# Linear attention feeding a gated MLP: features, keys and queries on half rows in pairs, TensorE in program order

## The chip, the cores and the metric

The kernel runs on one core of a Trainium2 chip. The metric is the device time of one execution in microseconds; lower is better. The core has five engines that run side by side and wait for each other through semaphores: TensorE (PE, with its weight loads shown apart as PEld), VectorE (DVE), ScalarE (ACT), GpSimd (POOL) and SyncE (SP). TensorE writes to PSUM, which has eight banks here; results are taken out of it by ScalarE or VectorE ("evacuated").

## The reference

Eight batches, eight heads, 576 positions, head size 64. First a linear attention with an exponential feature map, then an MLP with a spatial gate:

```python
def phi(x):
    proj = np.einsum('bhsd,df->bhsf', x, w_phi)             # 64 -> 128
    proj = proj - np.max(np.abs(proj), axis=-1, keepdims=True)
    return np.concatenate([np.exp(proj), np.exp(-proj)], axis=-1)
q_p, k_p = (phi(q), phi(k))
kv = np.einsum('bhsf,bhsd->bhfd', k_p, v)
z = np.sum(k_p, axis=2)
num = np.einsum('bhsf,bhfd->bhsd', q_p, kv)
den = np.einsum('bhsf,bhf->bhs', q_p, z)[..., None] + 1e-06
attn_out = num / den

x = attn_out.transpose(0, 2, 1, 3).reshape(B, S, 512)
h = np.maximum(x @ w_in, 0.0)                               # 512 -> 1024
u, v = h[..., :512], h[..., 512:]
v_n = (v - mean(v)) / np.sqrt(var(v) + 1e-06)
v_s = np.einsum('ts,bsd->btd', w_spatial, v_n) + b_spatial[None, :, None]
out = (u * v_s) @ w_out
```

## The kernel before

The attention works in *units*. A unit is one pair of heads of one batch over 512 positions (four blocks of 128), 32 in all, or, for two batches at a time, all eight heads over the last 64 positions (the *tail*), four in all. `step(i)` starts unit i and carries on with units started earlier, each part of the work at a fixed lag (`LAGS`): keys and queries at the unit's own step, maxima one step later, features and sums two later, attention three, output four.

- `a_transpose`: keys and queries with the head dimension on the partitions, two half rows (64 partitions each) one above the other. From batch 2 on a DMA does it (`cross`, tiles `kT_b`, `qT_b`).
- `a_keys` and `a_queries` call `by_token`: k or q times `w_phi`, positions on the partitions, one PSUM bank of 128x512 for each of two halves. `wphi2` is `w_phi` twice along a block diagonal, zeros elsewhere, so that one matmul over all 128 rows handles both half rows and gives 256 columns (L232). Of the keys VectorE takes the maximum of the absolute values (`mk`, L244) and ScalarE the exponentials with both signs (`kf`, L247). Of the queries VectorE takes the maximum (`mq`, L258), and GpSimd splits it into two bf16 parts (`mhl`, L261 and L262).
- `a_scale`: the key maximum becomes a factor `em` on v (`vs`, GpSimd, L272).
- `a_max_t`: `mhl` is transposed (L293) and copied to `mT` by VectorE (L294).
- `a_qfeat`: the query projection again, features on the partitions (L304; L313 for a tail), minus the maximum, which a matmul of the selection matrix `sel` with `mT` adds into the same bank (L308; L315). ScalarE takes both exponentials (`qf`, L321).
- `a_kv`: the sums over positions (L334, L336; evacuated as `kv`). `a_num`: numerator and denominator (L354), then division on VectorE (L344, L345) into `x`; `tail_num` does it for the tail (L382).
- `a_x_t`: the transpose of x, by a DMA for most units.

When a batch is complete, `b_tasks` appends its *second-stage tasks* to `queue`: v with the layer norm's statistics (`b_v`: matmuls L403, ScalarE relu L405, VectorE statistics L406, L407), the normalization on GpSimd (`b_ln`), u (`b_u`: L456, ScalarE relu L458), the spatial product (`b_s`: L477, L478, multiplied into u on VectorE, L480), and the output (`b_o`: L500, evacuated by ScalarE as `ob`, L502, written by a DMA of SP), and the same for tails. `fill(share)` adds `RATE * share` to a credit, up to `CAP`, and takes tasks off the queue while the credit covers half of the next task's cost, which is counted in us of TensorE (0.85 for four matmuls of 512 columns, 1.07 for five). The rest of the queue is emptied after the last step.

Engines and lines are chosen by the kernel. The order in which each engine's instructions stand is made by a scheduler from the order of the program, except where `tc.keep_in_program_order` holds an instruction to it. All PSUM tiles share one pool of eight banks; a tile waits for a bank whose last reader is done. The scheduler's order for the kernel before has, in a middle step on TensorE: maxima transpose, keys, a task, queries, a task, attention, sums, a task, features.

Of the kernel before, what the change touches and what calls it, by code (L numbers as in the profile page):

```python
# [16 lines left out]
def kernel(  # L17
# [15 lines left out]
    nc = tc.nc  # L33
# [23 lines left out]
    psum = ctx.enter_context(tc.tile_pool(name="psum", bufs=8, space=bass.MemoryType.PSUM))  # L57

# [65 lines left out]
    wphi2 = cpool.tile([P, 2 * F], BF16)  # L124
    pin(nc.vector.memset)(wphi2, 0.0)
# [14 lines left out]
    sel1 = cpool.tile([P, H], BF16)  # L140
    sel = cpool.tile([P, H, F], BF16)
    pin(nc.vector.tensor_tensor)(out=sel1, in0=ident[:, 0:H], in1=ident[:, H:2 * H], op=ALU.add)
    pin(nc.vector.tensor_scalar)(out=sel, in0=sel1.unsqueeze(2).to_broadcast([P, H, F]), scalar1=-1.0,
# [4 lines left out]
    for i in range(2):  # L148
        t = cpool.tile([P, 2, 2, H, DA], BF16, name=f"vst{i}")
        pin(nc.scalar.copy)(out=t.rearrange("p b s h d -> p (b s h d)"), in_=zero.to_broadcast([P, 4 * H * DA]))  # L150
        vst.append(t)
        if i == 0:
            for y in range(2):
                r = slice(y * D, (y + 1) * D)
                pin(nc.scalar.copy)(out=wphi2[r, y * F:(y + 1) * F], in_=wphi_f[r, :])
        t = cpool.tile([P, 2, HALF], BF16, name=f"vnt{i}")
        for bl, row in ((0, TL), (1, 0)):
            pin(nc.scalar.copy)(out=t[:, bl, :], in_=ident[:, row:row + 1].to_broadcast([P, HALF]))
        vnt.append(t)
# [24 lines left out]
    XX = 9  # L184
    EK = 7
    def transpose_spatial(i):

        pt = psum.tile([P, S], BF16, tag="bank", name="pt")
        if i < NB:
            sc = POS[i]  # L190
            for tp, c in enumerate(POS):
                nc.tensor.transpose(out=pt[:, tp * P:(tp + 1) * P], in_=wsp[:, c, bass.ds(sc, P, step=NB)],
                                    identity=ident)
            nc.tensor.transpose(out=pt[:, T0:S], in_=wspt[:, bass.ds(sc, P, step=NB)],
# [3 lines left out]
        for bl in range(2):  # L198
            lo = bl * TL
            for tp, c in enumerate(POS):  # L200
                nc.tensor.transpose(out=pt[lo:lo + TL, tp * P:(tp + 1) * P], in_=wspr[:, c, :], identity=ident)
            nc.tensor.transpose(out=pt[lo:lo + TL, T0:S], in_=wspt[:, T0:S], identity=ident[:TL, :TL])
# [9 lines left out]
    def a_transpose(u):  # L212
# [5 lines left out]
        for x, copy in (("k", nc.vector.tensor_copy if u["i"] < EK else nc.scalar.copy), ("q", nc.vector.tensor_copy)):  # L218
            pt = psum.tile([P, 4, P], BF16, tag="bank", name="pt")
            for j in range(4):  # L220
# [4 lines left out]
                nc.tensor.transpose(out=pt[:, j, :], in_=blk, identity=ident)  # L225
# [3 lines left out]
    def by_token(xT, half):  # L229
        ps = psum.tile([P, 4, F], FP32, tag="bank", name="ps")  # L230
        for x in range(2):
            nc.tensor.matmul(out=ps[:, 2 * x:2 * x + 2, :], lhsT=xT[:, 2 * half + x, :], rhs=wphi2,  # L232
                             start=True, stop=True)
        return ps

    def a_keys(u):

        u["mk"] = small.tile([P, H], FP32, tag="mk", name="mk")
        u["kf"] = feat.tile([P, 2, H, F], BF16, tag="kf" if u["pair"] else "kf_t", name="kf",
                            bufs=4 if u["pair"] else 2)  # L240
        for half in range(2):
            pk = by_token(u["kT"], half)
            hs = slice(4 * half, 4 * half + 4)
            nc.vector.tensor_reduce(out=u["mk"][:, hs], in_=pk, axis=AX.X, op=ALU.max,  # L244
                                    apply_absolute_value=True)
            for s, sc in ((0, 1.0), (1, -1.0)):
                nc.scalar.activation(out=u["kf"][:, s, hs, :], in_=pk, func=AF.Exp, bias=0.0, scale=sc)  # L247

    def a_queries(u):

        m, early = mhl[u["i"] % NM], u["i"] < EARLY
        if not early:
            mq = small.tile([P, H], FP32, tag="mq", name="mq")
        for half in range(2):
            pq = by_token(u["qT"], half)
            if early and half == 0:
                mq = pq[:, 0, 0:H]
            nc.vector.tensor_reduce(out=mq[:, 4 * half:4 * half + 4], in_=pq, axis=AX.X, op=ALU.max,  # L258
                                    apply_absolute_value=True)
        eng = nc.vector if early else nc.gpsimd  # L260
        eng.tensor_copy(out=m[:, 0:H], in_=mq)  # L261
        eng.tensor_tensor(out=m[:, H:2 * H], in0=mq, in1=m[:, 0:H], op=ALU.subtract)  # L262
# [28 lines left out]
    def a_max_t(u):  # L291
        pt = psum.tile([P, P], BF16, tag="bank", name="pt")
        nc.tensor.transpose(out=pt, in_=mhl[u["i"] % NM], identity=ident)  # L293
        nc.vector.tensor_copy(out=mT[u["i"] % NM][0:2 * H, :], in_=pt[0:2 * H, :])  # L294

    def a_qfeat(u):

        m = mT[u["i"] % NM]
        u["qf"] = []
        for half in range(2):  # L300
            pq = psum.tile([P, 4, P], FP32, tag="bank", name="pq")
            if u["pair"]:
                for par in range(2):
                    nc.tensor.matmul(out=pq[:, 2 * par:2 * par + 2, :], lhsT=wphi2[:, par * F:(par + 1) * F],  # L304
                                     rhs=u["qT"][:, 2 * half:2 * half + 2, :], start=True, stop=False)
                    for x in range(2):
                        j = 4 * half + 2 * x + par
                        nc.tensor.matmul(out=pq[:, 2 * par + x, :], lhsT=sel[:, j, :], rhs=m,  # L308
                                         start=False, stop=(x == 1))
            else:  # L310
                for x in range(4):
                    h = 4 * half + x
                    nc.tensor.matmul(out=pq[:, x, :], lhsT=wphi2[:, (h % 2) * F:(h % 2 + 1) * F],  # L313
                                     rhs=u["qT"][:, h // 2, :], start=True, stop=False)
                    nc.tensor.matmul(out=pq[:, x, :], lhsT=sel[:, h, :], rhs=m, start=False, stop=True)  # L315
            if u["pair"]:
                qf = feat.tile([P, 2, 4, P], BF16, tag="qf", name="qf", bufs=7)
            else:
                qf = feat.tile([P, 2, 4, P], BF16, tag="qf_t", name="qf_t", bufs=4)
            for s, sc in ((0, 1.0), (1, -1.0)):  # L320
                nc.scalar.activation(out=qf[:, s], in_=pq, func=AF.Exp, bias=0.0, scale=sc)  # L321
            u["qf"].append(qf)

    def a_kv(u):
# [5 lines left out]
        for hh in range(2):  # L330
            h = 2 * u["pj"] + hh
            for s in range(2):
                for c in range(NB):
                    nc.tensor.matmul(out=pv[:, hh, s, :], lhsT=u["kf"][:, s, 4 * hh + c, :],  # L334
                                     rhs=u["vs"][:, s, 4 * hh + c, :], start=(c == 0), stop=False)
                nc.tensor.matmul(out=pv[:, hh, s, :], lhsT=ut["kf"][:, s, h, :],  # L336
# [10 lines left out]
    def a_num(u):  # L347
        d = st[u["b"]]
        u["x"] = a1.tile([P, NB, 2, D], BF16, tag="x", name="x", bufs=3)
        for hh in range(2):  # L350
            pn = psum.tile([P, NB, DA], FP32, tag="bank", name="pn")
            for pos in range(NB):
                for s in range(2):
                    nc.tensor.matmul(out=pn[:, pos, :], lhsT=u["qf"][hh][:, s, pos, :],  # L354
# [3 lines left out]
    def a_x_t(u):  # L358
# [8 lines left out]
        for pos in range(NB):  # L367
            nc.tensor.transpose(out=pt[:, pos, :], in_=u["x"][:, pos].rearrange("p h d -> p (h d)"), identity=ident)
        nc.vector.tensor_copy(out=dst, in_=pt.rearrange("p n t -> p (n t)"))

    def tail_num(g, bls):
# [4 lines left out]
        for i in range(2):  # L376
            pn = psum.tile([P, 4, DA], FP32, tag="bank", name="pn")
            for y in range(4):
                for bl in bls:
                    r = slice(bl * TL, (bl + 1) * TL)  # L380
                    for s in range(2):
                        nc.tensor.matmul(out=pn[r, y, :], lhsT=qf[i][:, s, y, r],  # L382
# [5 lines left out]
    def tail_x_t(g, bls):  # L388
# [5 lines left out]
        for kc in range(KC):  # L394
            nc.tensor.transpose(out=pt[:, kc, r], in_=d["xt"][r, 2 * kc:2 * kc + 2, :].rearrange("p h d -> p (h d)"),
# [4 lines left out]
    def v_mm(lhs, dst, r, stats, mv):  # L400
        pv = psum.tile([P, HALF], FP32, tag="bank", name="pv")
        for kc in range(KC):
            nc.tensor.matmul(out=pv[r], lhsT=lhs(kc), rhs=w_in_bf[:, kc, HALF:DFF],  # L403
# [48 lines left out]
    def b_u(b, dc):  # L452
        d = st[b]
        pu = psum.tile([P, T0], FP32, tag="bank", name="pu")
        for kc in range(KC):
            nc.tensor.matmul(out=pu, lhsT=w_in_bf[:, kc, dc * P:(dc + 1) * P], rhs=d["xT"][:, kc, :],  # L456
# [3 lines left out]
    def b_u_tail(g, bls):  # L460
# [5 lines left out]
        for dc in range(KC):  # L466
            for kc in range(KC):
                nc.tensor.matmul(out=pu[:, dc, r], lhsT=w_in_bf[:, kc, dc * P:(dc + 1) * P],
# [215 lines left out]
```

## Time and profile before

| | |
|---|---|
| time before, three runs | 288.0, 289.58 (median), 291.42 us |
| span of the profiled execution | 286.4 us; what lies around it is not given |
| PE busy | 261.6 us (91%) |
| ACT busy | 229.3 us (80%) |
| DVE busy | 201.8 us (70%) |
| POOL busy | 182.2 us (64%) |
| granted TensorE clock | full throughout |

How to read it: busy time is the union of an engine's instructions, so overlapping ones count once, while the mean of a group is that of one instruction with its latency. The chain of waits follows the execution back from its last instruction, at each point to what released it. The timeline gives start, duration, engine, line, operation, output and input; a merged row has xN. Brackets name idle time ahead of an instruction and what ended it. The table by stretch gives the start and end of a stretch, its length, and then the busy time of PE, PEld, DVE, ACT and POOL with the number of instructions, the clock, the share of the DMA engines, and GB/s.

The span has four parts. Up to 18.7 us the first units are loaded and begun. From there to 49.4 us seven steps run with hardly any second-stage work. From 49.4 to 222.0 us lie 27 steps with second-stage tasks among them. The remaining 64.4 us hold the last steps, which have no new units, and the second stage of the last batches.

### The profile page before, as it was taken

Reading aid. Unit: us, or ns where it says so; the run is one execution under the profiler, and the core shown is the slowest. Engines: PE = TensorE matmul, PEld = TensorE weight load, DVE = VectorE, ACT = ScalarE, POOL = GpSimd, SP = SyncE. Lnnn points to the kernel's source line nnn. Section 1 sums busy time; section 2 is a strip of 40 time slices with the busy share of each in tenths; the row PEclk is TensorE's granted clock in tenths of the full one; section 3 lists DMA queues with packets and bytes.
Section 4 is the critical chain, followed back from the end, with each engine's and each line's share of the span. In section 5 each row is a group of like instructions: output and inputs, shape, how many; then the busy total and the mean of one; then the engine's idle time right before and its main releaser. Section 6 shows DMA issues by size and latency. Waiting matters only on the chain.

```text
span 286.4 us, 7965 instructions
## 1 busy us (share of the span) xinstructions
PE 261.6 (91%) x3070; PEld 178.6 (62%) x3070; DVE 201.8 (70%) x509; ACT 229.3 (80%) x517; POOL 182.2 (64%) x320
## 2 busy tenths in 40 slices
PE   1378889999999999999989999999999999999983
PEld 1157776777666776767557687666667676545441
DVE  4389997977958877598696887578688864354610
ACT  4949998899799988999998679799999746566033
POOL 8159998798336899479689954835969600058200
PEclk9999999999999999999999999999999999999999
DMA  6989999976568499999955994999111003500037
GB/s 185 203 171 120 206 219 223 163 203 71 79 147 186 102 187 155 173 245 196 130 94 102 225 191 87 264 287 255 32 22 32 7 2 122 211 3 0 0 90 242
DMA packets 81706, 40.31 MB, mean 141 GB/s; under 512 B 50242, under 2 KB 77058, under 8 KB 81668
## 3 DMA queue, kind: packets, MB, share of 16 engines
q1 hardware_dynamic: 54180, 28.32, 43.0%
q0 software_dynamic: 27328, 11.41, 35.5%
q8 instruction: 24, 0.39, 0.6%
q14 instruction: 14, 0.11, 0.2%
q10 hardware_dynamic: 160, 0.07, 0.1%
HBM read 32.85 MB, written 9.44 MB: 148 GB/s over the span
## 4 chain that ended last, share of the span: by engine, by line
PE 61%; ACT 14%; DVE 11%; DMA 9%; POOL 2%; issue 2%; ACTq 0%; SPq 0%; POOLq 0%; DVEq 0%
PE pv L403 10%; PE ps L477 8%; PE po L500 7%; PE pu L456 7%; PE ps L232 5%; ACT qf L321 5%; ACT kf L247 5%; PE pv L334 4%; DMA q_tl<-in_q_dram 4%; PE pn L354 4%; DMA out_dram<-ob 3%; PE pq L308 3%; PE pq L304 3%; DVE mk L244 3%; PE ps L478 2%; DVE mq L258 2%
## 5 line engine op out<-in xcount | busy, mean ns | idle before, releaser
L247 ACT ACTIVATE kf<-ps 128x512 bf16<-128x512 f32 x144 | 77.7, 692 | 5.6 <-DVE mk L244 5.4
L272 POOL TENSOR_TENSOR vs<-v_f,em 128x512 bf16<-128x512 f32 x64 | 65.6, 1049 | 23.6 <-ACT em L267 22.6
L321 ACT ACTIVATE qf<-pq 128x512 bf16<-128x512 f32 x128 | 68.2, 675 | 8.5 <-PE pq L308 8.5
L244 DVE TENSOR_REDUCE mk<-ps 128x4 f32<-128x512 f32 x72 | 46.1, 677 | 2.5 <-PE ps L232 2.0
L258 DVE TENSOR_REDUCE mq<-ps 128x4 f32<-128x512 f32 x62 | 39.9, 681 | 4.2 <-PE ps L232 3.4
L502 ACT COPY ob<-po 128x512 f32<-128x512 f32 (+1 forms) x37 | 21.6, 610 | 19.9 <-PE po L500 16.2
L406 DVE BATCH_NORM_STATS2 stats<-vr 128x6 f32<-128x512 bf16 (+1 forms) x37 | 24.8, 687 | 15.8 <-ACT vr L405 15.7
L477 PE MATMUL ps<-w_spT,vn 128*128 128x512 bf16 x128 | 32.8, 379 | 0.0
L456 PE MATMUL pu<-xT,w_in_bf 128*128 128x512 bf16 x128 | 31.6, 379 | 0.0
L403 PE MATMUL pv<-w_in_bf,xT 128*128 128x512 bf16 x128 | 31.2, 379 | 0.0
L480 DVE TENSOR_TENSOR uT<-ps,uT 128x512 bf16<-128x512 f32 x32 | 22.0, 689 | 12.7 <-PE ps L478 11.5
L500 PE MATMUL po<-w_out_bf,uT 128*128 128x512 bf16 x128 | 30.4, 379 | 0.0
L308 PE MATMUL pq<-mT,sel 128*128 128x128 bf16 x256 | 30.0, 219 | 0.0
L308 PEld LDWEIGHTS <-sel 128*128 128x128 bf16 x256 | 25.1, 98 | 3.9
L405 ACT ACTIVATE vr<-pv 128x512 bf16<-128x512 f32 (+1 forms) x37 | 23.3, 691 | 4.0 <-PE pv L403 3.9
L354 PEld LDWEIGHTS <-qf 128*128 128x128 bf16 x512 | 20.4, 97 | 8.2 <-issue 1.7
L345 DVE TENSOR_TENSOR x<-pn,rc 128x256 bf16<-128x256 f32 x64 | 25.0, 418 | 0.5
L420 POOL TENSOR_SCALAR vn<-vr,rs 128x512 bf16<-128x512 bf16 x32 | 24.3, 773 | 0.8
L334 PE MATMUL pv<-vs,kf 128*128 128x66 bf16 x512 | 24.5, 194 | 0.2 <-ACT kf L247 0.2
L354 PE MATMUL pn<-kv,qf 128*128 128x66 bf16 x512 | 22.3, 193 | 1.3 <-ACT qf L321 1.2
L334 PEld LDWEIGHTS <-kf 128*128 128x128 bf16 x512 | 21.7, 97 | 1.8 <-issue 0.9
L304 PE MATMUL pq<-qT_b,wphi 128*128 128x256 bf16 x96 | 22.4, 273 | 0.0
(120 smaller groups left out, 530.8 us busy)
## 6 DMA issues: line engine op xcount, KB each, us to landing
v_f<-in_v_dram SPq DMA_DIRECT2D x8, 1024.0 KB, 10.7
out_dram<-ob SPq DMA_DIRECT2D x32, 256.0 KB, 3.6
k_bf<-in_k_dram POOLq DMA_DIRECT2D x7, 512.0 KB, 7.0
q_bf<-in_q_dram POOLq DMA_DIRECT2D x7, 512.0 KB, 8.7
v_tl<-in_v_dram SPq DMA_DIRECT2D x8, 128.0 KB, 7.7
w_in_bf<-in_moe_w_in_dram POOLq DMA_DIRECT2D x2, 512.0 KB, 8.7
out_dram<-ob SPq DMA_DIRECT2D x8, 128.0 KB, 2.4
k_tl<-in_k_dram POOLq DMA_DIRECT2D x8, 64.0 KB, 6.8
```

The costliest lines, as they stand in the source:

```text
L244: nc.vector.tensor_reduce(out=u["mk"][:, hs], in_=pk, axis=AX.X, op=ALU.max, apply_absolute_value=True)
L247: nc.scalar.activation(out=u["kf"][:, s, hs, :], in_=pk, func=AF.Exp, bias=0.0, scale=sc)
L258: nc.vector.tensor_reduce(out=mq[:, 4 * half:4 * half + 4], in_=pq, axis=AX.X, op=ALU.max, apply_absolute_value=True)
L272: nc.gpsimd.tensor_tensor(out=vs[:, s, :, 0:D], in0=st[u["b"]]["v"][:, pj * H:(pj + 1) * H, :], in1=em[:, s, :].unsqueeze(2).to_broadcast( ...
L308: nc.tensor.matmul(out=pq[:, 2 * par + x, :], lhsT=sel[:, j, :], rhs=m, start=False, stop=(x == 1))
L321: nc.scalar.activation(out=qf[:, s], in_=pq, func=AF.Exp, bias=0.0, scale=sc)
L334: nc.tensor.matmul(out=pv[:, hh, s, :], lhsT=u["kf"][:, s, 4 * hh + c, :], rhs=u["vs"][:, s, 4 * hh + c, :], start=(c == 0), stop=False)
L354: nc.tensor.matmul(out=pn[:, pos, :], lhsT=u["qf"][hh][:, s, pos, :], rhs=d["kv"][:, 2 * u["pj"] + hh, s, :], start=(s == 0), stop=(s == 1))
L403: nc.tensor.matmul(out=pv[r], lhsT=lhs(kc), rhs=w_in_bf[:, kc, HALF:DFF], start=(kc == 0), stop=(kc == KC - 1))
L456: nc.tensor.matmul(out=pu, lhsT=w_in_bf[:, kc, dc * P:(dc + 1) * P], rhs=d["xT"][:, kc, :], start=(kc == 0), stop=(kc == KC - 1))
L477: nc.tensor.matmul(out=ps, lhsT=d["vn"][:, sp, cs], rhs=w_spT[:, sp, 0:T0], start=(sp == 0), stop=False)
L500: nc.tensor.matmul(out=po[r], lhsT=lhs(dc), rhs=w_out_bf[:, dc, :], start=(dc == 0), stop=(dc == KC - 1))
```

## The change

`wphi2` gives way to `wphi`, `w_phi` once on each half of the partitions without zeros. Each projection is a pair of matmuls over 64 rows, one on the upper and one on the lower half of the array's rows, into two different banks. Features, keys and queries of a step follow each other as one group (`p_features`, `p_keys`, `p_queries`), six banks together. In the features the `sel` matmuls come first and one matmul of 512 columns per half row follows. The selection matrix has four entries, repeated on both halves; `mT` is copied in all its rows. The blocks of a unit stand in a different order in `kf` and `qf`, which `slot` translates.

From step 8 (`STRICT`) on, every TensorE instruction is held to the order of the program. The evacuations of the group (`e_features`, `r_keys`, `e_keys`, `r_queries`) are called with four equal `fill(0.25)` among them and the other parts; the maxima's transpose comes last in a step, and the features first in the next. `RATE` goes from 3.12 to 3.35 and `CAP` from 2.11 to 2.5. `ob` is evacuated by VectorE, except after the last step (`drain`), when ScalarE does it as before.

```diff
+    strict = [False]
+    def on_pe(f, *a, **kw):
+        r = f(*a, **kw)
+        if strict[0]:
+            tc.keep_in_program_order(r)
+    def matmul(**kw):
+        on_pe(nc.tensor.matmul, **kw)
...
-    wphi2 = cpool.tile([P, 2 * F], BF16)
-    pin(nc.vector.memset)(wphi2, 0.0)
+    wphi = cpool.tile([P, F], BF16)
...
-    sel1 = cpool.tile([P, H], BF16)
-    sel = cpool.tile([P, H, F], BF16)
-    pin(nc.vector.tensor_tensor)(out=sel1, in0=ident[:, 0:H], in1=ident[:, H:2 * H], op=ALU.add)
+    sel1 = cpool.tile([P, 4], BF16)
+    sel = cpool.tile([P, 4, F], BF16)
+    pin(nc.vector.tensor_tensor)(out=sel1, in0=ident[:, 0:4], in1=ident[:, 4:8], op=ALU.add)
+    for i in (D, D + 4):
+        pin(nc.vector.tensor_tensor)(out=sel1, in0=sel1, in1=ident[:, i:i + 4], op=ALU.add)
...
-    def by_token(xT, half):
-        ps = psum.tile([P, 4, F], FP32, tag="bank", name="ps")
-        for x in range(2):
-            nc.tensor.matmul(out=ps[:, 2 * x:2 * x + 2, :], lhsT=xT[:, 2 * half + x, :], rhs=wphi2,
-                             start=True, stop=True)
-        return ps
+    HALVES = (slice(0, D), slice(D, P))
+    def banks(name):
+        return [psum.tile([P, 4, P], FP32, tag="bank", name=name) for par in range(2)]
+    def by_token(xT, name):
+        outs = banks(name)
+        for y in range(4):
+            for par, r in enumerate(HALVES):
+                matmul(out=outs[par][:, y, :], lhsT=xT[r, y, :], rhs=wphi[r, :], start=True, stop=True)
+        return outs
+    def p_features(u):
+        m = mT[u["i"] % NM]
+        u["pf"] = pf = banks("pf")
+        for y in range(4):
+            for par, r in enumerate(HALVES):
+                matmul(out=pf[par][:, y, :], lhsT=sel[r, y, :], rhs=m[r, :], start=(y == 0), stop=False)
+        for par, r in enumerate(HALVES):
+            matmul(out=pf[par], lhsT=wphi[r, :], rhs=u["qT"][r], start=False, stop=True)
+    def e_features(u):
+        u["qf"] = qf = feat.tile([P, 2, 8, P], BF16, tag="qf" if u["pair"] else "qf_t", name="qf",
+                                 bufs=3 if u["pair"] else 2)
+        for par in range(2):
+            for s, sc in ((0, 1.0), (1, -1.0)):
+                nc.scalar.activation(out=qf[:, s, 4 * par:4 * par + 4, :], in_=u["pf"][par], func=AF.Exp,
+                                     bias=0.0, scale=sc)
...
-        nc.vector.tensor_copy(out=mT[u["i"] % NM][0:2 * H, :], in_=pt[0:2 * H, :])
+        nc.vector.tensor_copy(out=mT[u["i"] % NM], in_=pt)
...
-        nc.scalar.copy(out=ob[r], in_=po[r])
+        (nc.scalar.copy if drain[0] else nc.vector.tensor_copy)(out=ob[r], in_=po[r])
...
-    ORDER = (("keys", 0.375), ("queries", 0.25), ("attention", 0), ("sums", 0.25),
-             ("next", 0.125), ("features", 0), ("out", 0), ("maxima", 0))
-    RATE = 3.12
-    CAP = 2.11
+    RATE = 3.35
+    CAP = 2.5
...
+        strict[0] = i >= STRICT
+        run("features", p_features)
+        run("keys", p_keys)
+        run("queries", p_queries)
+        run("features", e_features)
+        run("keys", r_keys, lambda u: e_keys(u, 0))
+        fill(0.25)
+        run("queries", r_queries)
+        run("keys", lambda u: e_keys(u, 1), a_scale)
+        fill(0.25)
+        for u in at_work("attention"):
+            a_num(u)
+            if u["pj"] == NP - 1:
+                finish_batch(u, tail_num)
+        fill(0.25)
+        run("sums", a_kv)
+        run("next", a_transpose)
+        fill(0.25)
+        for u in at_work("out"):
+            a_x_t(u)
+            if u["pj"] == NP - 1:
+                finish_batch(u, tail_x_t)
+                queue.extend(b_tasks(u["b"]))
+        run("maxima", a_max_t)
```

`r_keys` and `r_queries` are the two VectorE reductions of `a_keys` and `a_queries` over both banks (with `mhl` split by GpSimd as before), and `e_keys(u, par)` the two ScalarE exponentials of one bank. The old loop over `ORDER` in `step`, which called the parts and then `fill(share)`, is removed.

## The prediction

> **What bounds the kernel now.** I read, in this order: busy time per engine with the chain that ended last, busy time by stretch, the groups by line with shapes kept apart, the timeline of one step.
>
> ```profile
> PE 261.6 (91%) x3070; PEld 178.6 (62%) x3070; DVE 201.8 (70%) x509; ACT 229.3 (80%) x517; POOL 182.2 (64%) x320
> PE 61%; ACT 14%; DVE 11%; DMA 9%; POOL 2%; issue 2%; ACTq 0%; SPq 0%; POOLq 0%; DVEq 0%
> ```
>
> TensorE holds 61% of the chain, but ScalarE and VectorE follow at 80% and 70%. By stretch (length, then busy time of PE, PEld, DVE, ACT, POOL):
>
> ```profile
> 49.40:222.00 172.60, 169.19 (x2110) 119.55 (x2109) 135.47 (x335) 157.90 (x372) 126.71 (x228) 1.00 0.90 151
> 222.00:286.40 64.40, 59.18 (x534) 33.12 (x531) 29.00 (x67) 32.07 (x61) 17.24 (x32) 1.00 0.23 75
> 18.70:49.40 30.70, 26.47 (x393) 21.42 (x392) 28.10 (x81) 27.78 (x68) 29.27 (x44) 1.00 1.17 179
> ```
>
> In the middle, 27 steps between copies of mT, TensorE works 169.2 of 172.6 us. A step takes 172.6/27 = 6.4 us. VectorE has 37 us to spare, ScalarE 15.
>
> The groups that the change rewrites, and the evacuations that it re-orders (mean ns last):
>
> ```profile
> L247 ACT ACTIVATE kf<-ps 128x512 bf16<-128x512 f32 x144 | 77.7, 692 | 5.6 <-DVE mk L244 5.4
> L244 DVE TENSOR_REDUCE mk<-ps 128x4 f32<-128x512 f32 x72 | 46.1, 677 | 2.5 <-PE ps L232 2.0
> L308 PE MATMUL pq<-mT,sel 128*128 128x128 bf16 x256 | 30.0, 219 | 0.0
> L304 PE MATMUL pq<-qT_b,wphi 128*128 128x256 bf16 x96 | 22.4, 273 | 0.0
> L232 PE MATMUL ps<-wphi,qT_b 128*128 128x256 bf16 x96 | 14.5, 273 | 1.4 <-DMA qT_b<-q_bf 1.4
> L232 PE MATMUL ps<-wphi,kT_b 128*128 128x256 bf16 x96 | 14.4, 272 | 0.0
> ```
>
> These means overlap. I use pace: four L232 matmuls take 0.44 us in the chain (0.11 each), eight of 512 columns 1.73 (0.216 each), ScalarE's exponentials come 0.49 apart, VectorE's reductions 0.60 apart.
>
> One step in time order decides the forecast:
>
> ```profile
> 121.49 0.22 PE L293 MATMUL pt<-ident,mhl 128*128 128x128 bf16 x1
> 121.55 0.60 PE L232 MATMUL ps<-wphi,kT_b 128*128 128x256 bf16 x4
> 121.62 0.69 DVE L406 BATCH_NORM_STATS2 stats<-vr 128x6 f32<-128x512 bf16 x1 [2.23 <-ACT vr L405]
> 122.23 0.19 DVE L294 COPY mT<-pt 16x128 bf16<-16x128 bf16 x1
> 122.45 1.26 DVE L244 TENSOR_REDUCE mk<-ps 128x4 f32<-128x512 f32 x2
> 126.14 0.27 PE L304 MATMUL pq<-qT_b,wphi 128*128 128x256 bf16 x1
> ```
>
> Maxima are transposed at 121.49 and copied at 122.23. TensorE never waits: it starts keys at 121.55, and the features that read mT only at 126.14. That copy has nearly 4 us of slack, and the key matmuls lie between it and VectorE's next work.
>
> [...]
>
> ```profile
> 53.57 0.39 PE L192 MATMUL pt<-ident,wsp 128*128 128x128 bf16 x4
> 53.89 0.22 PE L194 MATMUL pt<-ident,wspt 64*128 64x64 bf16 x1
> 54.04 0.41 PE L192 MATMUL pt<-ident,wsp 128*128 128x128 bf16 x4
> ```
>
> Four at 0.055 us end their turn at 53.79; the 64-row one starts at 53.89, the next group 0.15 later: about 0.1 us per switch. [...] no 64-row pair is in this trace. [...]
>
> **The change part by part.**
>
> *Half rows in pairs.* Keys and queries: each 4 x 0.11 = 0.44 becomes 4 pairs x 0.055 = 0.22. Features: 4 x 0.11 + 8 x 0.055 = 0.88 becomes 4 pairs of sel x 0.055 + one pair of 512 columns 0.216 = 0.44. Saved: 0.88 a step if pairs overlap fully, nothing if they don't (the low bound); two switches take 0.2. I take a net 0.65 a step: 27 x 0.65 = 18 us in the middle.
>
> *The new wait.* In the built order every step from STRICT on reads: last second-stage task, maxima transpose, features, keys, queries; features begin with sel on mT. So TensorE waits for transpose (0.22), VectorE's copy (0.20) and two handovers (0.04 seen from pt to copy; about 0.1 back): 0.56 at least. VectorE's copy stands behind its evacuation of the step's last task wherever that is a spatial product or an output: 0.60 more, less what passes during the transpose, so about 1.1. Mean 0.85 a step, x 27 = 23 us. Behind it queue all TensorE work; VectorE's next instruction, mk, waits for keys behind features: 0.1 + 0.1 + 0.22 + 0.22 + 0.22 + 0.2 of pipeline = about 1.05 us idle each step. Slack is gone, and TensorE and VectorE take turns.
>
> *More tasks per step.* RATE 3.12 to 3.35 gives TensorE 0.23 more a step: 27 x 0.23 = 6 us in the middle. Late, the built order shows a spatial task, a spatial tail and one output fewer after the last maxima (1.07 + 1.2 + 0.86 = 3 us).
>
> *Outputs on VectorE.* 19 of the middle's steps' ob copies move. Their price there isn't shown: L227 (417 ns, bf16) bounds it below, L480 (689) above; I take 0.60, 11.4 us onto VectorE, some 10 off ScalarE. ScalarE's relief hides nothing by itself; VectorE's cover is the 37 us, which turn-taking consumes.
>
> *Middle, three sums.* TensorE: 169 - 18 + 6 + 23 = 180 to 182. VectorE: 135.5 + 11.4 + 2 for the extra tasks + 27 x 1.05 = 177. Neither is alone: a step with four layer-norm tasks asks VectorE for 2.4 + 1.0 + 0.13 + 4 x 0.7 + 1.05 = 7.3 us, and its statistics wait for ScalarE, which in the built order gives vr only after the key exponentials; a step with four uT tasks asks ScalarE for 12 x 0.49 + 0.75 = 6.6. Before, a heavy step ran on into a light one. Going through the 27 steps of the built order, taking each one's dearest engine, I get 186: 13.4 more than 172.6.
>
> *Early* (7 steps, not strict but in the same order): VectorE is busy 28.1 of 30.7, and 1.05 idle a step replaces about 0.4; with TensorE's gain I take +3 (bounds 0 and +5). *Late*: -3 of tasks, -0.9 for the features of two steps, +1 of waits: -3.
>
> *At nothing*: sel and wphi (one 0.29 us copy and half of a 0.72 us scaling less; the k_tl transfer, waited for until 12.89, covers them; uncovered, below 1 us); the mT copy of 128 rows for 16 (same columns); qf as one tile. No DMA changes in number. SP's order changes only in how outputs lie among xT transposes; POOL keeps its order of work, and the mhl that maxima read has a whole step. PSUM: six banks held could stall kv until the first key bank is free; by the built banks ScalarE frees it 3.8 us into a step, TensorE needs it at 4.3, so no cost; if ScalarE is late, up to 1 us a step.
>
> Sum: 286.4 + 13.4 + 3 - 3 = 299.8 us of span. What lies around the profiled span isn't given; the median shown, 289.58, is 3.2 above it. Some of the DMA waits of before (4.6 us for qT_b at 143 in the chain) should shrink in slower steps, so I add 2.2 rather than 3.2: **302 us**.
>
> **Rivals.**
>
> *A. Turn-taking costs more than pairs save* (above). For: 0.85 and 1.05 us against 0.65. Against: ScalarE may be the pace-setter, unaffected. Own range 292 to 311.
>
> *B. Faster: the boundary wait is absorbed.* If VectorE reaches the mT copy as soon as the transpose ends and the wait per step stays under the 0.65 us that pairs save, TensorE gains. Fully hidden: 289.6 - 18 in the middle - 3 early + 6 - 3 = about 272; half hidden, 281. For: VectorE's and ScalarE's totals would fit in 155 us only just (148 for ScalarE after outputs leave). Against: the built order puts evacuations ahead of the copy.
>
> *C. Pairs don't overlap* (the change doesn't do what it says): the group takes 0.88 longer in each of some 34 steps, partly under ScalarE: 302 + 15 to 25 = 317 to 327. [...]
>
> *D. Even*: wait and saving cancel, 287 to 292.
>
> **How the numbers follow.** A 0.64, B 0.20, C 0.07, D 0.09. About 1% (2.9 us) is what a measurement can tell. A has a little below 292.5: faster 0.20, same 0.11, slower 0.69. The range leaves out B's lower half and C: 279 to 316.
>
> **What would show it.** Right: an idle of 0.5 to 1.1 us on PE ahead of sel with mT as releaser, in each step; VectorE waiting about 1 us ahead of mk for pk; [...] ob on DVE near 0.60; middle step 6.9 us. Wrong: PE ahead of sel idle under 0.3; pairs spaced like whole ones (C); steps under 6.2 us (B); or most of the loss in waits for PSUM banks, which I priced at nothing.

## The result, and the profile after

| | before | after |
|---|---|---|
| time, median (lowest to highest) | 290.5 us (288.0 to 296.49, 4 runs) | 323.24 us (322.06 to 324.72, 4 runs) |
| ratio after to before | | 1.117, 95% interval 1.109 to 1.125 |
| profiled span | 286.4 us | 320.2 us |
| mean granted TensorE clock | 1.00 | 0.952 |
| early part, to step 8 | 49.4 us | 54.9 us |
| middle, 27 steps from one mT copy to the next | 172.7 us | 202.2 us |
| late part | 64.4 us | 63.1 us |

Ratios, here and below, leave out runs in a slower state, 1.5% or more above a kernel's fastest (here the 296.49), so they differ a little from ratios of the medians shown.

The direction was forecast, the size was not: 302 us, range 279 to 316. Almost all that is lost, 29.5 us, is lost in the 27 middle steps, for which 13.4 had been forecast.

The page of the kernel after: busy time by engine, the granted clock in 40 slices (tenths of full speed), the chain that ended last.

```profile
PE 253.0 (79%) x3270; PEld 158.3 (49%) x3270; DVE 217.3 (68%) x538; ACT 215.3 (67%) x488; POOL 180.6 (56%) x320
...
PEclk9999797979959899999899999998999999999999
...
PE 42%; DVE 23%; ACT 20%; DMA 7%; issue 4%; POOL 3%; SPq 0%; DVEq 0%; ACTq 0%; POOLq 0%
```

Before, TensorE was busy for 91% of the span and held 61% of the chain. Now no engine is busy for four fifths, and VectorE and ScalarE hold 43% of the chain between them: the work passes from one engine to the next. The clock, 1.00 throughout before, falls to 0.50 in episodes that a slice shows as a 5, a 7 or an 8.

The waits of the kernel after (us in total, times, longest):

```profile
ACT qf L277 <- PE pf L62: 61.3, 32, 6.4
...
PE pf L62 <- DVE mT L337: 38.4, 35, 3.5
DVE mk L286 <- PE pk L62: 34.3, 32, 1.9
...
DVE stats L421 <- ACT vr L420: 11.7, 10, 3.5
...
DVE ob L517 <- PE po L62: 7.0, 8, 2.0
```

In almost every step all three engines stand still once: TensorE for mT (38.4/35 = 1.10 us each), then ScalarE for the features and VectorE for the keys. Before, TensorE never waited for mT, and the other two waits were small:

```profile
ACT qf L321 <- PE pq L308: 8.5, 9, 1.2
...
DVE mk L244 <- PE ps L232: 2.0, 1, 2.0
```

By stretch (length, then busy time of PE, PEld, DVE, ACT, POOL, then the clock):

```profile
54.89:257.09 202.20, 167.41 (x2283) 104.59 (x2282) 148.62 (x358) 151.66 (x357) 128.06 (x233) 0.95 0.78 128
...
54.89:124.95 70.06, 58.01 (x716) 35.36 (x716) 47.90 (x118) 48.44 (x112) 39.55 (x74) 0.90 0.65 107
161.50:170.83 9.33, 7.55 (x87) 4.28 (x87) 7.14 (x21) 8.70 (x22) 6.12 (x15) 1.00 0.71 115
...
204.25:222.69 18.44, 13.37 (x170) 7.70 (x169) 13.17 (x33) 10.46 (x24) 9.71 (x18) 0.91 1.13 236
```

The loss isn't spread evenly. The first eight middle steps (70.06 us) and the two from 204.25 on (18.44) take 8.85 us each, 2.17 more than the same steps before (52.56 and 14.28 us):

```profile
49.38:101.94 52.56, 52.33 (x654) 37.09 (x653) 42.03 (x109) 47.75 (x113) 36.25 (x67) 1.00 0.78 144
177.86:192.14 14.28, 13.39 (x165) 9.12 (x164) 9.15 (x23) 12.62 (x30) 9.59 (x17) 1.00 1.16 272
```

The other seventeen take (202.20 - 70.06 - 18.44)/17 = 6.69, which is 0.47 more than their 6.22 before. In each step, copy to copy, take the busy time of the busiest of TensorE, VectorE and ScalarE, and add these up: before, that gives 170.9 of 172.7 us; after, 174.0 of 202.2. In the ten heavy steps it is 72.4 of 88.5. So in the changed kernel a step is no longer filled by its busiest engine.

The longest of the ten, from one mT copy to the next, holds spatial products and a tail's output:

```profile
81.67 0.21 DVE L337 COPY mT<-pt 128x128 bf16<-128x128 bf16 x1
...
82.58 2.06 ACT L277 ACTIVATE qf<-pf 128x512 bf16<-128x512 f32 x4 [2.04 <-PE pf L62]
...
82.81 1.29 DVE L286 TENSOR_REDUCE mk<-pk 128x4 f32<-128x512 f32 x2 [0.93 <-PE pk L62]
...
88.49 0.42 DVE L510 TENSOR_TENSOR uTt<-ps,uTt 128x256 bf16<-128x256 f32 x1
88.97 1.92 PE L62 MATMUL po<-w_out_bf,uTt 128*64 128x512 bf16 x4 [1.89 <-DVE uTt L510]
...
90.92 0.68 DVE L517 COPY ob<-po 64x512 f32<-64x512 f32 x1 [2.01 <-PE po L62]
91.53 0.41 DVE L384 COPY xT<-pt 128x512 bf16<-128x512 bf16 x1
91.86 0.21 DVE L337 COPY mT<-pt 128x128 bf16<-128x128 bf16 x1
```

Read it as one chain. From the mT copy through features and keys to mk: 1.14 us. Then VectorE works through its queue until uTt is done at 88.91: 6.10. TensorE waited for that, and its four matmuls and the handovers take 2.01. VectorE evacuates ob, copies xT, and only then reaches the next mT copy: 0.94. Together 10.19, the length of the step, while no engine is busy for more than 7.71 (TensorE). The ten don't share one kind of task: the step from 54.89 holds layer-norm work, the one from 204.25 outputs.

The longest of the seventeen is full of layer-norm work:

```profile
161.50 0.21 DVE L337 COPY mT<-pt 128x128 bf16<-128x128 bf16 x1
...
162.69 2.16 ACT L277 ACTIVATE qf<-pf 128x512 bf16<-128x512 f32 x4
...
168.14 1.29 ACT L420 ACTIVATE vr<-pv 128x512 bf16<-128x512 f32 x2
...
169.10 0.22 PE L62 MATMUL pt<-ident,mhl 128*128 128x128 bf16 x1
...
170.03 0.66 DVE L421 BATCH_NORM_STATS2 stats<-vr 128x6 f32<-128x512 bf16 x1
...
170.83 0.19 DVE L337 COPY mT<-pt 128x128 bf16<-128x128 bf16 x1
171.08 0.40 PE L62 MATMUL pf<-mT,sel 64*128 64x128 bf16 x8 [1.75 <-DVE mT L337]
```

From the mT copy to qf pass 1.19 us, in which ScalarE still finishes work of the step before; qf, kf, em and five vr keep it until 169.43 (6.74); VectorE gets the last vr's statistics done and only then reaches the mT copy, although its input is there from 169.3 on (1.40). Here ScalarE is busy 8.70 of the 9.33 us, so this step is nearly filled by one engine.

### The profile page after: what moved, and what is told of

It reads as the page before. It is cut to its first block, busy times and chain, and to the rows that moved or that the text cites. A ratio compares the mean times of both kernels' runs of the same rounds, so it can differ in the third digit from the quotient of the medians.

```text
span 320.2 us, 8370 instructions
## 1 busy us (share of the span) xinstructions
PE 253.0 (79%) x3270; PEld 158.3 (49%) x3270; DVE 217.3 (68%) x538; ACT 215.3 (67%) x488; POOL 180.6 (56%) x320
## 4 chain that ended last, share of the span: by engine, by line
PE 42%; DVE 23%; ACT 20%; DMA 7%; issue 4%; POOL 3%; SPq 0%; DVEq 0%; ACTq 0%; POOLq 0%
PE ps L62 11%; ACT qf L277 10%; PE pf L62 7%; PE pv L62 7%; PE po L62 6%; ACT kf L291 6%; PE pu L62 5%; DVE stats L421 4%; DMA q_tl<-in_q_dram 4%; DMA out_dram<-ob 3%; DVE mk L286 3%; DVE x L360 3%; PE pn L62 2%; DVE ob L517 2%; DVE uT L495 2%
## 5 line engine op out<-in xcount | busy, mean ns | idle before, releaser
L277 ACT ACTIVATE qf<-pf 128x512 bf16<-128x512 f32 x144 | 74.8, 618 | 61.3 <-PE pf L62 61.3
L291 ACT ACTIVATE kf<-pk 128x512 bf16<-128x512 f32 x144 | 79.3, 663 | 4.3 <-DVE mk L286 4.2
L286 DVE TENSOR_REDUCE mk<-pk 128x4 f32<-128x512 f32 x72 | 46.4, 686 | 36.5 <-PE pk L62 34.3
L62 PE MATMUL pf<-mT,sel 64*128 64x128 bf16 x288 | 15.6, 232 | 39.7 <-DVE mT L337 38.4
L299 DVE TENSOR_REDUCE mq<-pq 128x4 f32<-128x512 f32 x62 | 40.5, 680 | 0.1
L62 PE MATMUL ps<-w_spT,vn 128*128 128x512 bf16 (+1 forms) x256 | 38.8, 286 | 1.4 <-POOL vn L435 1.0
L62 PEld LDWEIGHTS <-qf 128*128 128x128 bf16 (+1 forms) x640 | 24.1, 102 | 8.2 <-issue 1.7
L62 PE MATMUL pn<-kv,qf 128*128 128x66 bf16 (+1 forms) x640 | 26.0, 197 | 0.6 <-ACT qf L277 0.5
L517 DVE COPY ob<-po 128x512 f32<-128x512 f32 (+1 forms) x28 | 18.9, 685 | 9.4 <-PE po L62 7.0
L330 POOL TENSOR_TENSOR vst<-v_tl,em 64x512 bf16<-64x512 f32 x16 | 16.4, 1038 | 15.1 <-ACT em L310 14.8
```

What stands on the lines that cost most here:

```text
L62: r = f(*a, **kw)
L277: nc.scalar.activation(out=qf[:, s, 4 * par:4 * par + 4, :], in_=u["pf"][par], func=AF.Exp, bias=0.0, scale=sc)
L286: nc.vector.tensor_reduce(out=mk[:, par, :], in_=u["pk"][par], axis=AX.X, op=ALU.max, apply_absolute_value=True)
L291: nc.scalar.activation(out=u["kf"][:, s, 4 * par:4 * par + 4, :], in_=u["pk"][par], func=AF.Exp, bias=0.0, scale=sc)
L299: nc.vector.tensor_reduce(out=mq[:, 4 * par:4 * par + 4], in_=pq[par], axis=AX.X, op=ALU.max, apply_absolute_value=True)
L517: (nc.scalar.copy if drain[0] else nc.vector.tensor_copy)(out=ob[r], in_=po[r])
```

## The experiments

Theories. **W**: the engines take turns at mT, and the turn sets the length of a step. **L**: ScalarE's or VectorE's sum sets it. **K**: TensorE's clock falls because it idles, and that costs the time. **O**: ob on VectorE. **S**: TensorE in strict program order. The kernel before ran beside each group; its median lay between 289.2 and 293.9 us. So runs are compared by their ratio to it, with the 95% interval in brackets; the changed kernel's is 1.117 [1.109, 1.125].

### One part of the change undone or moved

**The wait.** Maxima moved from the end of a step to a place ahead of the attention:

```diff
         fill(0.25)
+        run("maxima", a_max_t)
         for u in at_work("attention"):
...
-        run("maxima", a_max_t)
```

> The changed kernel with one move: the maxima are transposed ahead of the attention instead of last in the step, so that VectorE can copy mT while TensorE has attention, sums and two tasks to do. If turn-taking at mT is the loss (theory W): PE's idle ahead of sel, 38.4 us in the changed kernel, falls under 8 us, VectorE's idle ahead of mk stays at some 30 (keys still come after features), and the time falls by 20 to 35 us, to 288 to 303. If VectorE and ScalarE are the real limit and the wait only shows it (theory L): the idle moves to waits for PSUM banks or other operands, and the time stays within 8 us of 323.

Measured: 300.85 us, 1.045 [1.034, 1.056]. Its waits:

```profile
ACT qf L277 <- PE pf L62: 26.5, 22, 5.4
...
DVE mk L286 <- PE pk L62: 9.6, 14, 1.9
DVE ob L517 <- DMA out_dram<-ob: 9.5, 4, 6.0
```

TensorE's wait for mT is gone (0.3 us is left), and with it more than half of the other two. This one line is worth 7.2 points of ratio, some 21 us of the 33. It is the largest piece.

**The order inside the group**: keys and queries ahead of the features, maxima still last.

> The changed kernel with the group in the order keys, queries, features; maxima still last in the step. Keys and queries (0.45 us) then run while VectorE copies mT, and VectorE gets keys 0.45 us earlier, while ScalarE gets features 0.45 us later. W: VectorE's idle ahead of mk falls from 34 us to under 15, PE's idle at mT from 38 to about 22, time down by 10 to 18 us. L, or ScalarE as the limit: no gain or up to 5 us worse.

Measured: 308.72 us, 1.072 [1.060, 1.084]. Two sets of matmuls now cover part of the copy: TensorE's wait for mT falls to 14.2 us. W again; but the wait changes its place:

```profile
ACT kf L291 <- DVE mk L286: 41.9, 24, 6.0
```

**ob by ScalarE throughout**, as before:

```diff
-        (nc.scalar.copy if drain[0] else nc.vector.tensor_copy)(out=ob[r], in_=po[r])
+        nc.scalar.copy(out=ob[r], in_=po[r])
```

> The changed kernel with ob evacuated by ScalarE throughout, as before the change. If the 28 ob copies on VectorE (18.9 us busy) lengthen VectorE's turn (theory O): down by 8 to 14 us. If turn-taking is set elsewhere in those steps: within 4 us of 323.

Measured: 320.41 us, 1.113 [1.097, 1.128].

**Not strict** (`STRICT = 1000`):

> The changed kernel (323.2 us) without the strict order of TensorE; the built order is nearly the same. Theory S (strict order costs 1 to 2 per cent here too): 316 to 320. Theory W (the turn at mT sets the step, and what TensorE waits for elsewhere is hidden in it): 320 to 325.

Measured: 320.72 us, 1.112 [1.109, 1.115].

**The old rate and cap of tasks** (3.12 and 2.11):

> The changed kernel with the rate of tasks 3.12 and the cap 2.11 of before. Of its 27 middle steps the ten heavy ones (the first eight, and those at 204 and 213 us) are 16 us over the forecast, the other seventeen are on it. Theory H (a step overfilled with tasks costs more than it saves at the end): 314 to 319. If tasks are worth the same wherever they stand: 321 to 327.

Measured: 318.62 us, 1.104 [1.096, 1.111]. These three ratios lie 0.4, 0.5 and 1.3 points below the changed kernel's, but all three intervals touch its own. What each is worth in this kernel isn't shown.

### The granted clock

One group of features, keys and queries in the changed kernel at full clock, and the next one, 5 us later:

```profile
152.00 0.40 PE L62 MATMUL pf<-mT,sel 64*128 64x128 bf16 x8 [0.32 <-DVE mT L337]
152.24 0.38 PE L62 MATMUL pf<-qT,wphi 64*128 64x512 bf16 x2
152.45 0.39 PE L62 MATMUL pk<-wphi,kT_b 64*128 64x128 bf16 x8
152.67 0.39 PE L62 MATMUL pq<-wphi,qT_b 64*128 64x128 bf16 x8
...
157.30 0.61 PE L62 MATMUL pf<-mT,sel 64*128 64x128 bf16 x8 [1.08 <-DVE mT L337]
157.68 0.66 PE L62 MATMUL pf<-qT_b,wphi 64*128 64x512 bf16 x2
158.10 0.66 PE L62 MATMUL pk<-wphi,kT_b 64*128 64x128 bf16 x8
```

At full clock a set of pairs starts 0.22 us after the one before; at 157.30, behind an idle of 1.08 us, 0.4. By stretch the clock there is 0.50 from 157.30 to 160.50. Length times (1 - clock), summed over the span, is 320.2 x 0.048 = 15 us, the most that TensorE can have lost. Does the clock fall because TensorE idles, and does that cost the kernel so much? TensorE was kept busier by matmuls whose result nobody reads, behind each maxima transpose, where TensorE waits for mT anyway:

```diff
         run("maxima", a_max_t)
+        if strict[0]:
+            w = psum.tile([P, T0], FP32, tag="bank", name="warm")
+            for j in range(3):
+                matmul(out=w, lhsT=ident, rhs=sel.rearrange("p y f -> p (y f)"), start=True, stop=True)
```

> The changed kernel with three matmuls of 512 columns more (0.65 us at full clock) between the maxima transpose and the features in each strict step, into a bank that nobody reads: they fill most of TensorE's idle time at mT, and otherwise cost 27 x 0.65 = 18 us at most. If the drops of the granted clock (mean 0.952) come of that idling and cost time (theory K): the clock goes to 0.98 or more and the time falls by 3 to 10 us. If the clock has nothing to do with it: the clock stays at 0.95, the time rises by 0 to 8 us.

Measured: 321.02 us, 1.116 [1.101, 1.132], mean clock 0.973. Then from step 2 on, six matmuls in a step that isn't strict and three in one that is:

> The changed kernel with TensorE kept busier: 3 matmuls of 512 columns into an unread bank behind the maxima in each strict step (as in e5_warm, 321.0 us, clock 0.973) and 6 in each early step from step 2 on. Theory K (the granted clock is a cause: in the changed kernel 15 us of TensorE time were lost to it, 5 of them in the early steps): clock above 0.98 and 312 to 318. Theory W (TensorE's speed matters little while the engines take turns; in e5_warm a gain of 0.02 in clock gave 0 to 2 us): 319 to 325.

Measured: 322.62 us, 1.118 [1.108, 1.127]. Its clock:

```profile
core 0: 321.9 us, clock 0.984
```

With TensorE busier the mean clock rose from 0.952 to 0.973 and 0.984. Two thirds of the lost clock came back (320 x (0.984 - 0.952) = 10 us), and nothing of the time as a whole. The added matmuls mostly fit into the idle time: three take 3 x 0.216 = 0.65 us, 30 of the 36 idle times ahead of sel are longer, and TensorE's wait there falls from 38.4 to 15.2 us.

Step by step, the two traces say more. Many steps that ran at full clock in the changed kernel agree within 0.03 us: there TensorE's own time is covered by its wait. Six of its middle steps hold a stretch at 0.50. Five of them, of 9.62, 10.20, 8.35, 7.71 and 4.47 us, take 8.51, 9.53, 7.76, 6.09 and 3.87 with the matmuls added, together 4.6 less; the sixth, of 9.14, takes 9.12. In the chain above, too, the four matmuls at 88.97 took 1.92 us at half clock; four of 512 columns take 1.02 at full clock, at 207.75. But the eighth middle step takes 11.49 us in place of 8.49. VectorE waits there 3.29 us for the first spatial product, against 1.66 in the changed kernel. In the run with only the three in a strict step, where this step takes 11.47 us, TensorE waits for GpSimd's normalization ahead of spatial products four times in the first eight middle steps (2.0 us), against three times (1.0) in the changed kernel. So K can be part of what makes heavy steps long, some 5 us of the 29.5, but raising the clock did not shorten the kernel.

### What the pairs are worth

**Full rows in the new order.** The changed kernel with `wphi` and `sel` padded with zeros to 128 rows, so that the same matmuls run one after another:

```diff
-                matmul(out=outs[par][:, y, :], lhsT=xT[r, y, :], rhs=wphi[r, :], start=True, stop=True)
+                matmul(out=outs[par][:, y, :], lhsT=xT[:, y, :], rhs=wphi[:, par, :], start=True, stop=True)
```

> The changed kernel with its new order, rate, strict order and ob by VectorE, but features, keys and queries on 128 rows as before (weights and selectors padded with zeros, so that the same matmuls run on full rows one after another): no pairs and no tiling switches. Theory W (the step is bound by the turn TensorE -> ScalarE/VectorE -> maxima -> TensorE, and the pairs shorten the TensorE part of that turn): +0.66 a step (0.88 less two switches of 0.1) x 34 = +22 us: 338 to 348 us. Theory L (ScalarE and VectorE set the step, TensorE has slack): 320 to 328, as after.

Measured: 336.87 us, 1.166 [1.159, 1.173]. The sets here start 0.45, 0.43, 0.45 and 0.45 us apart (medians of a late stretch); in the changed kernel 0.23, 0.22, 0.22 and 0.33, the last followed by a matmul on full rows. So the pairs do overlap and save TensorE 1.78 - 1.00 = 0.78 us a step, less the way in (about 0.1 us, below). Over 36 units that is up to 28 us; 14 came in, at a lower clock (0.952, with full rows 0.984).

**Pairs alone.** The kernel before with its order, rate, ob by ScalarE and no strict order, with features, keys and queries in pairs:

> The kernel before (its order of a step, its rate of tasks, ob by ScalarE, no strict order) with one thing of the change: features, keys and queries on half rows in pairs. The pairs no longer stand together, so that TensorE goes into and out of 64-row tiles about six times a step, not twice. Theory P (pairs are worth 0.88 us a step when they overlap, a switch costs about 0.1): 0.88 - 0.6 = 0.3 us a step, about 10 us in all: 280 to 286 us. If switches cost nothing or the switch is hidden: 0.88 x 34 = 30 us less at most, but VectorE and ScalarE stand beside TensorE in this kernel (135 and 158 of 169 us in the middle), so not below 272. If ScalarE bounds the step now (theory L): 288 to 293, no change. If the switches cost more than 0.2 each: above 295.

Measured: 289.79 us (20 runs), 1.001 [0.997, 1.004]. No gain at all, though TensorE is relieved. The middle of that run by stretch:

```profile
51.37:224.46 173.09, 164.87 (x2260) 94.60 (x2258) 134.44 (x336) 157.50 (x372) 125.57 (x227) 1.00 0.97 148
```

Before, TensorE was busy 169.2 of 172.6 us, now 164.9 of 173.1. So two things happen. The saving on TensorE shrinks to 4.3 us, since the sets stand apart and each pays its own way in and out: the keys' set starts 0.16 us after the transpose ahead of it (129.07 to 129.23), with full rows before 0.06 (121.49 to 121.55), and the keys' and the queries' next matmul starts after 0.33 us, not 0.22. And what is left of it turns into idle time.

Three variations of that run. Strict order from step 8 on:

> Run e6_pairs_alone (289.8 us) with TensorE in program order from step 8 on, and nothing else. Theory S: 294 to 300, some 0.2 to 0.4 us a step for waits that another order walks round. Theory G: 288 to 292, no difference.

Measured: 292.59 us, 1.012 [1.006, 1.019]: S, but small. Ob by VectorE:

> Run e6_pairs_alone (289.8 us) with ob by VectorE until the end, as in the change. ScalarE is busy 157.5 of 173.1 us in that run's middle, VectorE 134.4, and TensorE idles 8 us. Theory L (the pairs saved TensorE some 4 to 7 us that ScalarE then takes): with about 19 copies of 0.6 us moved away, 283 to 287. If it is the turn between engines, or VectorE's queue, and no one engine's sum: 289 to 294.

Measured: 292.82 us, 1.010 [1.006, 1.014]. To move 0.6 us a copy from ScalarE to VectorE makes it slower, not faster; ScalarE's sum alone is not the bound. Rates of 3.35 (with the cap 2.5) and of 2.9:

> Run e6_pairs_alone (ratio 1.0007) with the rate 3.35 and the cap 2.5. In that run's middle TensorE idled 8 us of 173, 5 more than before; the late part is TensorE's (57 of 64 us). If the time that pairs free can take tasks: 6 us of tasks move forward and the end is 2 to 5 us earlier, ratio 0.983 to 0.995. Theory L (ScalarE and VectorE stand at the pace already): 0.995 to 1.01.

> Run e6_pairs_alone (ratio 1.0007) with the rate 2.9 in place of 3.12. The rate 3.35 gave 1.0155. If the middle is set by ScalarE and VectorE and a fuller step only disturbs it: ratio 0.985 to 0.997. If 3.12 is near the best (the end then gets 6 us more of tasks on TensorE): 1.00 to 1.02.

Measured: 293.07 us, 1.016 [1.011, 1.020], and 304.04 us, 1.058 [1.048, 1.068]. Both are worse: the old rate is near the best, and the freed TensorE time in the middle takes no more tasks.

### The new order without the wait

Maxima ahead of the attention, and ob by ScalarE:

> Maxima before the attention (run e1_maxima_early, 300.9 us) and ob by ScalarE as before the change. Left over in that run were waits of VectorE on an output DMA (9.5 us in 4 waits at ob) and of TensorE on ob (5.6). Theory O (those waits hold TensorE in program order): 291 to 296. Theory K (what is left is the granted clock, 0.966 in that run, as the early steps still idle): 298 to 302. If ScalarE, which gets 26 x 0.6 us of work more, becomes the bound: 303 to 308.

Measured: 298.69 us, 1.034 [1.027, 1.042], not told apart from the run with the maxima moved alone. With the old rate as well:

> The run before this one with the rate of tasks 3.12 and the cap 2.11 of the kernel before. If tasks were pulled too early into the steps (0.23 us of tasks a step more, less left for the end): middle shorter by 27 x 0.2 = 5 us, end longer by as much: no change within 3 us. If a fuller step sets off waits on ScalarE: 3 to 8 us less than the run before this one.

Measured: 301.19 us, 1.041 [1.035, 1.048]. From this run, strict order taken away:

> Run e9_maxima_early_ob_scalar_rate (301.2 us) without the strict order of TensorE: the group, the maxima before the attention, ob by ScalarE, tasks at 3.12 and 2.11 as before. It differs from e6_pairs_alone (289.8) only by the order of a step. Theory S (what is left of the loss is TensorE standing in program order behind waits on uTt, vn, mhl and ob, some 10 us in that run's middle): 291 to 296. Theory G (it is the group itself, three sets at the head of a step that hold six of eight PSUM banks and leave VectorE and ScalarE nothing beforehand): 298 to 303.

Measured: 295.61 us, 1.020 [1.010, 1.029]: strict order costs 2.1 points here, some 6 us. What is left over the kernel with pairs alone, some 5 us, belongs to the order of the step. Over the same 27 steps TensorE is relieved of 9.5 us (159.7 busy, 169.2 before), and the middle is 7 us longer (179.7 us, 172.7 before):

```profile
46.41:226.12 179.71, 159.72 (x2264) 98.89 (x2262) 135.35 (x342) 160.49 (x375) 125.93 (x231) 0.99 0.96 147
```

Or is it the six PSUM banks that the group takes? In the run with the old rate, the queries' set was moved out of the group to a fill later, so that four banks are taken at once:

> Run e9_maxima_early_ob_scalar_rate (301.2 us) with the queries' set taken out of the group and put where its maxima are taken, a fill later: four PSUM banks are taken at the head of a step, not six, and two more tiling switches of about 0.1 us come in each step (+7 us of TensorE at most). Theory B (six of eight banks at once are what costs): 292 to 297. If banks are free anyway: 300 to 306.

Measured: 299.75 us, 1.036 [1.029, 1.042], no difference that the intervals show. At last, full rows in the run without strict order:

> Run e10_no_strict (295.6 us, ratio 1.0198: grouped, maxima before the attention, no strict order) with features, keys and queries on full rows, the same matmuls one after another, as in e7_full_rows. The pairs save TensorE 0.66 us a step there. If pairs pay wherever the group stands at the head of a step, because VectorE and ScalarE wait for it: 12 to 22 us slower, ratio 1.06 to 1.095. If they pay only by shortening the turn at mT: within 5 us, ratio 1.015 to 1.037.

Measured: 299.3 us, 1.038 [1.031, 1.046], just above the second answer and below the first: pairs are worth some 5 us here. So pairs are worth nothing in the old order (where they also save TensorE less), about 5 us in the group, and 14 where the group stands inside the turn at mT.

Taken one after another, these runs lead from the changed kernel back to the one before. The wait at mT is worth 7.2 points of ratio, ob and rate together 0.4 (within the noise), strict order 2.1, the order of the step 1.9, and the pairs 0.1 (none). Undone in another sequence, the parts would come out differently: strict order alone gave 0.5. No version was found that beats the kernel before.

## Why the prediction was wrong

**What bounds the kernel before**: TensorE's 169.2 of 172.6 us was read as TensorE being the bound, with 15 us to spare on ScalarE. Relieved of 4 us (pairs alone), it idles, and the middle stays at 173; relieved of 9.5 in another order, it idles more. So it isn't the bound by itself. ScalarE's 15 us are an average: in 15 of the 27 steps before, ScalarE too was busy for over 98% of the step.

**Half rows in pairs, net 0.65 a step**: right as TensorE time (0.78 less about 0.1 for the way in). That the two matmuls of a pair overlap was the author's assumption, which no trace of the kernel before showed; in the changed kernel sets start 0.22 us apart, on full rows 0.45. Wrong as time of the kernel: 18 us were booked in TensorE's sum for the middle, while the changed kernel gains some 14 in the whole, and the old order none.

**The new wait**: there as described, and somewhat larger. In the middle TensorE waited 29.9 us, 1.11 on average (0.32 to 3.5) over the 27 steps, against 23 and 0.85 (from 0.56 to 1.1); VectorE waited 25.4 us ahead of mk, against 28. From the end of an mT copy to sel passed 0.06 us (171.02 to 171.08), against about 0.1. Undoing the wait gave back 21 to 22 us.

**More tasks**: right. By the matmuls recorded, tasks of the middle took TensorE some 5 us more (23 matmuls of 512 columns at 0.216), against 6.

**Outputs on VectorE**: 0.60 apart as taken; cost within the noise of the run that undid it. A wait of VectorE for an output's DMA (2.3 us, in the step from 204.25) wasn't forecast.

**The middle, three sums**: this is the step that failed. "Going through the 27 steps of the built order, taking each one's dearest engine, I get 186" gave 13.4 us; 29.5 were measured. In seventeen steps the length was near the 6.9 of the forecast's mean. In the ten heavy ones it is 16.1 us over the busy time of the busiest engine: the length is the chain from one mT copy to the next, which passes from engine to engine. In the step shown it took 10.19, with no engine busy for more than 7.71. For a step with four layer-norm tasks the forecast had VectorE's 7.3 us. The one shown took 9.33, of which ScalarE was busy 8.70: there the dearest engine itself was mistaken. The forecast saw TensorE and VectorE take turns and gave ScalarE no wait; it became the one that waits longest, 45.8 us in the middle ahead of qf. TensorE's own sum came to 167.4 busy and 34.8 idle in place of 157 and 23 to 25. Nearly all of the 10 us more of busy time can be the clock (202.2 x 0.05), a term that the forecast didn't have; some 5 us of it may show in the length of steps.

**Not strict, strict**: the strict order was priced at nothing apart from what the built order showed. It cost 1.1 and 2.1 points in two other orders; in the changed kernel itself its 2.5 us are within the intervals.

**Early, late**: +5.5 and -1.3 us, against +3 and -3. What makes up the early excess wasn't settled; a busier TensorE didn't remove it.

**PSUM banks at nothing**: the one test of it, four banks at once in the order without the wait, showed no difference. **The mT copy at nothing**: right, 0.211 us in the median for 128 rows, 0.202 for 16 before. **Rivals**: C fell (pairs start 0.22 apart a set), B fell (the wait is exposed in 35 steps), D fell.

**The range**: its upper end, 316, rests on the same dearest-engine sum, so the same fault was in both.

Open: why the new order without wait and strict order is still 2 per cent slower than pairs in the old order; and of the ten heavy steps only one was followed as a chain here.

## What to carry to other kernels

When a change puts an instruction that needs another engine's result at the head of a step, price the step as one chain from that handover to the next, through every engine's queue in order, not as the largest of the engines' sums; heavy steps show the difference (ten of them 88.5 us here, against 72.4). An engine that is 98% busy isn't thereby the bound (relieved of 4.3 us alone, TensorE left the middle at 173): relieve it alone and see whether the stretch gets shorter, and look at the others step by step, since an average hides the steps that they fill. A transpose or copy that the next step begins with belongs ahead of the long work of this one (7.2 points of ratio here).

## What the runs showed of the hardware

In the changed kernel the clock fell to 0.50 eight times between the first load and the last output, seven times for 3.41 us and once for twice that; in the 3.41 us ahead of each, TensorE was busy for 24 to 55%. It fell without one long idle: from 153.5 to 157.3 us TensorE was busy 1.96 of 3.8 us, in pieces, and its longest idle was 1.08 us; from 157.3 to 160.5 the granted clock was 0.50. And a set of four 64-row pairs followed by another set took 0.22 us, one followed by a full-row matmul 0.33, so that a group of three sets paid for its way out once.
